# Left rows of a linear attention in full 128-partition tiles, with the first weights' loads moved into the attention

## The chip, the cores and the metric

The kernel runs on one core of one Trainium2 chip. The metric is the device time of one execution in microseconds; times are medians of several executions, and one further execution was taken with the hardware profiler.

## What is computed

```
kv  = einsum('bhsd,bhse->bhde', k, v)          # b 4, h 8, s 576, d 64, all f32
out = einsum('bhsd,bhde->bhse', q, kv)
x   = out / sqrt(mean(out*out, -1) + 1e-6) * g_norm
x   = x.transpose(0, 2, 1, 3).reshape(2304, 512)
x   = softplus(x @ w1) @ w2                    # w1 512 x 2048, w2 2048 x 512
out = leaky_relu(x @ w3, 0.01) @ w4            # the same shapes
```

`softplus` and `leaky_relu` stand for the two expressions of the reference. The two layers after the attention are called the MLPs below.

## The kernel before, in words

The attention is worked off in 16 units: unit u is one batch b and one pair of heads (NU = 4 x 4). The 576 rows of a batch are 4 x 128 rows, and 64 rows that are left (RL = 64). For each unit `load` asks for q, k and v of the 512 rows (256 KB each, a ring of five, line 368), and with a batch's first pair for the 64 left rows of all eight heads (128 KB each, a ring of two, line 377). All these loads, and those of the weights, are asked for by SyncE's queue (SP), in one order.

What a unit does on TensorE (PE): `T(u)` transposes q in four 128x128 blocks (line 400) and the left 64 rows (line 404), then sums k-transposed times v over four blocks of 128 rows (line 408) and over the left 64 rows (line 411). Lines 345 and 347 copy q and k to the layout for this, on VectorE (DVE), ScalarE (ACT) or GpSimd (POOL). The sum is masked (line 426, DVE) to `kvm`, the transposed q goes to `qt` (line 358 on DVE, 356 on ACT). `O(u)` multiplies `qt` by `kvm`: four blocks (line 439), and the left rows (line 445). `normal(w)` takes two units together, w = 0 to 7: squares (line 459, ACT), their sums (line 464, DVE), a reciprocal root, and the scaled rows `xn` (four blocks) and `xnl` (left rows, both line 501, DVE). `X(u)` transposes these back (line 523, and line 535 for the left rows) into `xy`, the input of the first MLP.

In the tiles of the left rows everything has 64 partitions: `ldr` and `xnl` are 64 partitions high, line 404 transposes 64 rows with a 64x64 identity, line 411 contracts over 64 partitions, line 445 writes 64 output rows, line 535 transposes 64 rows.

The first MLP's weights arrive as 64-bit numbers that are taken apart by bit operations (`decode_w`, lines 562 to 597, "chunks" of 512 KB) and then split in a high and a low part (`split_pair`, lines 636 to 669). Chunks 0 and 1 make the first pair, 2 and 3 the second. Their products (line 888) are laid between the later units of the attention as soon as four blocks of `xy` are there, and the MLPs' own products (lines 813, 961, 977) follow.

The order on each engine is not written by hand. `Plan` collects all operations with a cost and a due time, which grows with the PE work that was entered before the operation, and at each step gives each engine the operation that can start and is due first. A due time can be set by hand: `due=4 * no + 10` for the first four chunks (line 573). The planner fixes the order; on the chip each engine works its list off in that order and waits for semaphores.

Of the kernel before, what the change touches and what calls it, by code (L numbers as in the profile page):

```python
# [19 lines left out]
class Plan:  # L20
# [15 lines left out]
        self.readers = {}  # L36
        self.pe = 0.0

    def op(self, cost, fn, reads=(), writes=(), due=None):
        o = {"cost": cost, "fn": fn, "succ": [], "n": len(self.ops)}  # L40
        deps = {}
        for k in reads:
            if k in self.writer:
                deps[self.writer[k]["n"]] = self.writer[k]
        for k in writes:
            for d in [self.writer.get(k), *self.readers.get(k, ())]:
                if d is not None:
                    deps[d["n"]] = d
        for k in reads:
            self.readers.setdefault(k, []).append(o)  # L50
        for k in writes:
            self.writer[k], self.readers[k] = o, []
        o["deps"] = list(deps.values())
        for d in o["deps"]:
            d["succ"].append(o)
        o["due"] = self.pe
        if "PE" in cost:
            self.pe += cost["PE"]
        else:
            o["due"] += self.AHEAD  # L60
        if due is not None:
            o["due"] = due
        self.ops.append(o)
        return o

# [66 lines left out]
def linear_attention_two_mlps(  # L132
# [32 lines left out]
    nc = tc.nc  # L165
    B, H, S, D = q.shape
    NT, DM = out.shape
    DFF = w1.shape[1] // 2
    P = 128
    KC = DM // P  # L170
    NF = DFF // P
    RL = S - 4 * P
# [29 lines left out]
    def ring(pool, name, n, shape, dt=F32):  # L202
        return [pool.tile(shape, dt, name=f"{name}{i}") for i in range(n)]

    ident = const.tile([P, P], F32, name="ident")
# [97 lines left out]
    attp = att.__enter__()  # L303
    NLD = 5
    lda = {nm: ring(attp, nm + "a", NLD, [P, 2, 4, D]) for nm in "qkv"}
    ldr = {nm: ring(attp, nm + "r", 2, [RL, H, D]) for nm in "qkv"}
    qp = ring(attp, "qp", 2, [P, 4, 2, D])
    kp = ring(attp, "kp", 2, [P, 4, 2, D])
    qt = ring(attp, "qt", 2, [P, S])
# [1 line left out]
    sq = ring(mstp, "sq", 2, [P, 8, D])  # L311
    sql = ring(mstp, "sql", 1, [RL, 4, D])
    xn = ring(mstp, "xn", 4, [P, 8, D])
    xnl = ring(mstp, "xnl", 2, [RL, 4, D])

    ss = ring(mstp, "ss", 2, [P, 20])
    fa = ring(mstp, "fa", 2, [P, 20])
    fm = ring(mstp, "fm", 2, [P, 20])
    for t_ in ss:
        nc.vector.memset(t_, 1.0)  # L320

    plan = Plan()
    op = plan.op
# [39 lines left out]
    def load(u):  # L363
        b, hp = u // NPAIR, u % NPAIR
        hs = slice(2 * hp, 2 * hp + 2)
        for nm, src in (("q", q), ("k", k), ("v", v)):
            def fn(e, nm=nm, src=src):
                nc.sync.dma_start(  # L368
                    out=lda[nm][u % NLD],
                    in_=src[b, hs, 0:4 * P, :].rearrange("h (p r) d -> p h r d", r=4),  # L370
                )

            op({"S": 0.73}, fn, (), [(nm, u % NLD)])
        if hp == 0:
            for nm, src in (("q", q), ("k", k), ("v", v)):
                def fn(e, nm=nm, src=src):
                    nc.sync.dma_start(
                        out=ldr[nm][b % 2], in_=src[b, :, 4 * P:S, :].rearrange("h p d -> p h d")
                    )

                op({"S": 0.73}, fn, (), [(nm + "r", b % 2)])

    def T(u):
        b, hp = u // NPAIR, u % NPAIR
        h2 = slice(2 * hp, 2 * hp + 2)
        i = u % 2
        for nm, dst in (("q", qp), ("k", kp)):
            copy_to(
                dst[i], lda[nm][u % NLD].rearrange("p h r d -> p r h d"), 512,
                [(nm, u % NLD)], [(nm + "p", i)],  # L390
            )
        p0 = 2 * i if u < U_H else 0
        p1 = p0 + 1
        kv = ps[p1][:, 2 * P:3 * P]
        ql, kl, vl = (ldr[nm][b % 2] for nm in "qkv")
        va = lda["v"][u % NLD]

        def f_t(e, j):
            for r in range(2):
                nc.tensor.transpose(  # L400
                    ps[p0 + j][:, r * P:(r + 1) * P], qp[i][:, 2 * j + r, :, :], ident
                )
            if j == 0:
                nc.tensor.transpose(ps[p0][:, 2 * P:2 * P + RL], ql[:, h2, :], ident[:RL, :RL])  # L404

        def f_kv(e):
            for r in range(4):
                nc.tensor.matmul(  # L408
                    kv, kp[i][:, r, :, :], va[:, :, r, :], start=(r == 0), stop=False
                )  # L410
            nc.tensor.matmul(kv, kl[:, h2, :], vl[:, h2, :], start=False, stop=True)  # L411

        for j in range(2):
            n = (2 * P + RL, 2 * P)[j]
            c0 = (0, 2 * P + RL)[j]
            op(
                {"PE": 0.25}, lambda e, j=j: f_t(e, j),
                [("qp", i)] + ([] if j else [("qr", b % 2)]), [("ps", p0 + j)],
            )
            if j:  # L420
                op(
                    {"PE": 1.1}, f_kv,
                    [("kp", i), ("v", u % NLD), ("kr", b % 2), ("vr", b % 2)], [("ps", p1)],
                )
                op(
                    {"D": 0.22}, lambda e: nc.vector.tensor_tensor(kvm[i], kv, mask, ALU.mult),
                    [], [("ps", p1), ("kvm", i)],
                )
            from_psum(qt[i][:, c0:c0 + n], ps[p0 + j][:, :n], n, p0 + j, [("qt", i, j)])
# [3 lines left out]
    def O(u):  # L433
        i = u % 2
        at_ = (0, P, 2 * P + RL, 3 * P + RL)

        def f_o(e):
            for r in range(4):
                nc.tensor.matmul(  # L439
                    ps[4 + i][:, r * P:(r + 1) * P], qt[i][:, at_[r]:at_[r] + P], kvm[i],  # L440
                    start=True, stop=True,
                )

        def f_l(e):
            nc.tensor.matmul(  # L445
                ps[6][:RL, i * P:(i + 1) * P], qt[i][:, 2 * P:2 * P + RL], kvm[i],
                start=True, stop=True,
            )

        need = [("kvm", i), ("qt", i, 0)]  # L450
        op({"PE": 0.87}, f_o, need + [("qt", i, 1)], [("ps", 4 + i)])
        op({"PE": 0.22}, f_l, need, [("ps", 6)])
        squares(ps[4 + i], ("ps", 4 + i), sq[i], ss[u // 2 % 2][:, 8 * i:8 * i + 8], ("sq", i),
                ("ss", u // 2 % 2, i), P, 8)
# [14 lines left out]
    def normal(w):  # L469
# [18 lines left out]
        def newton(e):  # L488
# [5 lines left out]
        parts = [  # L494
            (xn[2 * i + t], ps[4 + t], m_[:, 8 * t:8 * t + 8], ("ps", 4 + t), ("xn", 2 * i + t), P, 8)
            for t in range(2)
        ] + [(xnl[i], ol, m_[:RL, 16:20], ("ps", 6), ("xnl", i), RL, 4)]
        for x_, o, r_, ok, xk, p, n in parts:
            op(
                {"D": t_d(n * D)},  # L500
# [16 lines left out]
    def X(u):  # L517
        b, hp = u // NPAIR, u % NPAIR
        i = u % 2

        def f_x(e):
            for r in range(4):
                nc.tensor.transpose(  # L523
                    ps[7][:, r * P:(r + 1) * P], xn[u % 4][:, 2 * r:2 * r + 2, :], ident
                )

        cm, cl = (b * S + RL, b * S) if b % 2 else (b * S, b * S + 4 * P)
        op({"PE": 0.44}, f_x, [("xn", u % 4)], [("ps", 7)])
        scaled(xy[:, hp, cm:cm + 4 * P], ps[7], 4 * P, 7, xyk([hp], cm, 4 * P))
        if i == 0:  # L530
            return

        def f_l(e):
            for t in range(2):
                nc.tensor.transpose(  # L535
                    ps[6][:, 2 * P + t * RL:2 * P + (t + 1) * RL],
                    xnl[u // 2 % 2][:, 2 * t:2 * t + 2, :], ident[:RL, :RL],
                )

        op({"PE": 0.11}, f_l, [("xnl", u // 2 % 2)], [("ps", 6)])  # L540
        scaled(
            xy[:, hp - 1:hp + 1, cl:cl + RL],
            ps[6][:, 2 * P:2 * P + 2 * RL].rearrange("p (a n) -> p a n", a=2),
            2 * RL, 6, xyk([hp - 1, hp], cl, RL),
        )

# [3 lines left out]
    def decode_w(F, which, a_reg):  # L550
# [1 line left out]
        src = ((w1, w2), (w3, w4))[ph][which]  # L552

        ri = chunk_no[0] % 2 if chunk_no[0] >= 6 else chunk_no[0] % 2 * 2
        no = chunk_no[0]
        chunk_no[0] += 1
        r, t_ = raw[ri], sqr

# [10 lines left out]
                )  # L569

        rk, tk, ak = r.keys(), [("sqr",)], a_reg.keys()

        op({"S": 1.46}, f_l, (), rk, due=4 * no + 10 if no < 4 else None)
        op(
            {"A": t_a(DM)},
            lambda e: nc.scalar.activation(  # L576
# [22 lines left out]
    def decode_pair(F, which, i):  # L599

        for m in range(2):
            decode_w(F + m, which, half[i][m])
# [426 lines left out]
        {"D": 0.08}, lambda e: nc.vector.tensor_scalar(gcol, graw, -0.5, None, ALU.mult),  # L1029
        [("graw", 0), ("graw", 1)], [("gcol",)],  # L1030
    )
    for f in range(2):
        decode_pair(2 * f, 0, 0)
        split_pair(0, f, True)
    for i in range(NU + XL):
        if i < NU:
            T(i)
            if i + NLD < NU:
                load(i + NLD)
        if i >= XL:  # L1040
            X(i - XL)
            if i - XL == 2 * NPAIR - 1:
                first_blocks()
                decode_pair(0, 1, 0)
        if 1 <= i <= NU:
            O(i - 1)
            if i % 2 == 0:
                normal(i // 2 - 1)
# [103 lines left out]
```

## Time and profile before

| | us |
|---|---|
| median of 3 runs | 844.09 (843.69 to 844.68) |
| the profiled execution, whole | 841.17 |
| its span in the profile | 839.4 |
| PE busy | 824.8 (98%) |
| DVE busy | 578.1 (69%) |
| ACT busy | 447.8 (53%) |
| POOL busy | 65.6 (8%) |

The profiled execution took 841.17 us, 1.8 us more than the span that the profile shows, and 2.9 us less than the median of the runs. An engine's busy time is an average over an attention of some 97 us and MLPs of some 742 us. A busy PE need not be PE at its peak, since the ends of matmuls are modelled; the distance from the start of one matmul to the start of the next is what PE took for it.

### The profile page before, as it was taken

How to read it: one execution, taken by the hardware profiler on the slowest of the kernel's cores; microseconds unless marked ns; L12 is line 12 of the kernel's file. 1: busy time of each engine (PE TensorE's matmuls, PEld its weight loads, DVE VectorE, ACT ScalarE, POOL GpSimd, SP SyncE). 2: the span in 40 equal slices, each digit the busy share in tenths (PEclk: the TensorE clock that was granted, in tenths of full speed). 3: DMA queues.
4: the chain of work that ended last, by engine and by line, in shares of the span. 5: the costliest groups of instructions: out<-in, count | busy, mean ns of one | idle time of the engine just before them, and what ended most of it. 6: DMA issues, size and time to landing. Idle time of an engine off the chain costs nothing.

```text
span 839.4 us, 11949 instructions
## 1 busy us (share of the span) xinstructions
PE 824.8 (98%) x4524; PEld 772.0 (92%) x4524; DVE 578.1 (69%) x928; ACT 447.8 (53%) x725; POOL 65.6 (8%) x116
## 2 busy tenths in 40 slices
PE   6999999999999999999999999999999999999997
PEld 4788999999999999999999988989889889889886
DVE  6887988878468665867688886766378754753342
ACT  4644976866355544555466565565364554453330
POOL 3321000000100100000000000010010010010000
PEclk9999999999999999999999999999999999999999
DMA  9981565376645752764866965764654852543613
GB/s 309 342 271 64 201 244 188 145 251 211 222 135 162 248 204 72 249 202 158 302 209 212 324 252 191 253 221 134 210 168 135 286 176 65 200 152 100 200 51 100
DMA packets 78712, 164.08 MB, mean 195 GB/s; under 512 B 11456, under 2 KB 54208, under 8 KB 78656
## 3 DMA queue, kind: packets, MB, share of 16 engines
q1 hardware_dynamic: 67136, 100.42, 35.7%
q0 software_dynamic: 11520, 62.92, 22.6%
q8 instruction: 35, 0.57, 0.3%
q14 instruction: 21, 0.17, 0.1%
HBM read 132.25 MB, written 31.06 MB: 195 GB/s over the span
## 4 chain that ended last, share of the span: by engine, by line
PE 96%; DVE 1%; DMA 1%; ACT 1%; SPq 0%; issue 0%; ACTq 0%; DVEq 0%
PE ps L813 40%; PE ps L961 24%; PE ps L977 24%; PE ps L439 2%; PE ps L408 2%; PE ps L888 2%; PE ps L400 1%; PE ps L523 1%; DMA qr<-in_q_dram 1%; PE ps L411 1%; PE ps L445 1%; PE ps L404 0%; DVE xy L691 0%; PE ps L535 0%; SPq L368 0%
## 5 line engine op out<-in xcount | busy, mean ns | idle before, releaser
L813 PE MATMUL ps<-ra 128*128 128x384 f32 x1932 | 387.8, 335 | 0.0
L813 PEld LDWEIGHTS ps<-ra 128*128 128x128 f32 x1932 | 342.8, 188 | 14.0
L961 PE MATMUL ps<-rb 128*128 128x384 f32 x1152 | 226.6, 334 | 0.0
L977 PE MATMUL ps<-rb 128*128 128x512 f32 x864 | 224.7, 393 | 0.0
L961 PEld LDWEIGHTS ps<-rb 128*128 128x128 f32 x1152 | 202.1, 188 | 0.0
L921 DVE TENSOR_TENSOR mf<-ps,mf 128x384 f32<-128x384 f32 x138 | 76.7, 556 | 165.6 <-PE ps L813 134.3
L977 PEld LDWEIGHTS ps<-rb 128*128 128x128 f32 x864 | 159.8, 188 | 23.7
L914 ACT ACTIVATE mf<-ps 128x384 f32<-128x384 f32 x138 | 67.8, 492 | 109.4 <-PE ps L813 108.2
L691 DVE TENSOR_TENSOR xy<-ps,xy 128x384 f32<-128x384 f32 (+1 forms) x126 | 77.3, 614 | 29.1 <-PE ps L977 20.8
L796 POOL DMA_DIRECT2D ra<-xscr x80 | 42.8, 536 | 672.3 <-PE ps L813 652.8
L847 DVE TENSOR_TENSOR rb<-mf,rb 128x768 fp32r<-128x768 f32 x96 | 91.3, 951 | 3.9 <-ACT rb L842 3.8
L842 ACT ACTIVATE rb<-mf 128x768 fp32r<-128x768 f32 x96 | 81.3, 847 | 2.7
L719 ACT ACTIVATE ra<-mf 128x768 fp32r<-128x768 f32 x63 | 53.0, 841 | 27.7 <-PE ps L813 26.7
L714 DVE TENSOR_TENSOR ra<-mf,ra 128x768 fp32r<-128x768 f32 x63 | 60.1, 955 | 11.0 <-ACT ra L719 10.7
L834 ACT ACTIVATE mf<-mf 128x768 f32<-128x768 f32 (+1 forms) x48 | 32.8, 683 | 61.6 <-DVE mf L921 61.6
L828 ACT ACTIVATE mf<-mf 128x768 f32<-128x768 f32 (+1 forms) x48 | 33.3, 694 | 45.1 <-DVE mf L921 45.0
L686 ACT ACTIVATE xy<-ps 128x384 f32<-128x384 f32 (+1 forms) x35 | 18.5, 528 | 15.1 <-PE ps L961 10.8
L588 DVE SCALAR_TENSOR_TENSOR sqr<-mf,sqr 128x512 int32<-128x512 int32 x35 | 24.4, 696 | 0.8
L594 DVE SCALAR_TENSOR_TENSOR mf<-mf,sqr 128x512 int32<-128x512 int32 x34 | 24.0, 706 | 0.4
L576 ACT ACTIVATE mf<-mf 128x512 f32<-128x512 f32 x20 | 13.4, 669 | 17.1 <-DMA mf<-in_moe_w_in_dram 13.7
L400 PE MATMUL ps<-ident,qp 128*128 128x128 f32 x64 | 13.3, 306 | 8.6 <-POOL qp L347 7.8
L582 DVE TENSOR_SCALAR sqr<-mf 128x512 int32<-128x512 int32 x34 | 15.4, 453 | 8.1 <-ACT mf L576 7.5
(85 smaller groups left out, 606.6 us busy)
## 6 DMA issues: line engine op xcount, KB each, us to landing
ra<-xscr POOLq DMA_DIRECT2D x80, 768.0 KB, 6.0
mf<-xscr SPq DMA_DIRECT2D x51, 384.0 KB, 5.5
mf<-in_moe_w_in_dram SPq DMA_DIRECT2D x18, 512.0 KB, 4.8
xscr<-ra SPq DMA_DIRECT2D x12, 768.0 KB, 3.8
xscr<-rc SPq DMA_DIRECT2D x12, 768.0 KB, 4.6
mf<-in_moe_w_out_dram SPq DMA_DIRECT2D x17, 512.0 KB, 4.3
lf<-in_moe_w_out_dram SPq DMA_DIRECT2D x15, 512.0 KB, 3.5
xscr<-xy SPq DMA_DIRECT2D x19, 384.0 KB, 4.1
```

Of the source, the lines that this page charges most:

```text
L691: {"D": t_d(n)}, lambda e: nc.vector.tensor_tensor(dst, src, dst, ALU.add),
L714: ENG[e].tensor_tensor(e_[:, 1, :, :], src(), e_[:, 0, :, :].bitcast(F32), ALU.subtract)
L719: {"A": t_a(n)}, lambda e: nc.scalar.activation(e_[:, 0, :, :], src(), AF.Copy),
L796: lambda e: nc.gpsimd.dma_start(out=flat(xe[i]).ap, in_=xscr[7 * tp + i]),
L813: nc.tensor.matmul(o, w_[:, a, c:c + P], e_[:, b, kk, :], start=(not on and kk == 0 and n == 0), stop=(kk == 1 and n == 2), skip_group_che ...
L828: {"A": t_a(n)}, lambda e: nc.scalar.activation(dst(), src(), AF.Softplus),
L842: {"A": t_a(n)}, lambda e: nc.scalar.activation(g[:, 0, :, :], c.ap, AF.Copy),
L847: lambda e: nc.vector.tensor_tensor(g[:, 1, :, :], c.ap, g[:, 0, :, :].bitcast(F32), ALU.subtract),
L914: {"A": t_a(BN)}, lambda e: nc.scalar.activation(c[:, m, :], src, AF.Copy),
L921: lambda e: nc.vector.tensor_tensor(c[:, m, :], src, c[:, m, :], ALU.add),
L961: nc.tensor.matmul(y[:, :BN], w_[m][:, a, js], G_[:, b, m, :], start=(u == 0 and m == 0 and i == 0), stop=(u == 1 and m == 1 and i == 2),)
L977: nc.tensor.matmul(y, G_[:, a, m, js], w_[m][:, b, :], start=(u == 0 and m == 0 and i == 0), stop=(u == 1 and m == 1 and i == 2),)
```

## The change

Two edits. The tiles of the left rows are made 128 partitions high: the upper 64 partitions of the six `ldr` and the two `xnl` are set to zero once at the start, on DVE, and lines 404, 411, 445 and 535 work on 128 partitions, or 128 output rows. The product of line 445 now reads 64 columns of `qt` that belong to another block, so it also waits for the second half of `qt`; the rows that come of them are not used. Second, the decoding and splitting of the first two pairs of chunks are entered with units 1 and 3 of the attention, where before they were entered ahead of unit 0 with due times set by hand.

```
-    def op(self, cost, fn, reads=(), writes=(), due=None):
+    def op(self, cost, fn, reads=(), writes=()):
...
-        if due is not None:
-            o["due"] = due
...
-    ldr = {nm: ring(attp, nm + "r", 2, [RL, H, D]) for nm in "qkv"}
+    ldr = {nm: ring(attp, nm + "r", 2, [P, H, D]) for nm in "qkv"}
...
-    xnl = ring(mstp, "xnl", 2, [RL, 4, D])
+    xnl = ring(mstp, "xnl", 2, [P, 4, D])
...
+    for t_ in [t for n in "qkv" for t in ldr[n]] + xnl:
+        nc.vector.memset(t_[RL:], 0.0)
...
-                        out=ldr[nm][b % 2], in_=src[b, :, 4 * P:S, :].rearrange("h p d -> p h d")
+                        out=ldr[nm][b % 2][:RL], in_=src[b, :, 4 * P:S, :].rearrange("h p d -> p h d")
...
-                nc.tensor.transpose(ps[p0][:, 2 * P:2 * P + RL], ql[:, h2, :], ident[:RL, :RL])
+                nc.tensor.transpose(ps[p0][:, 2 * P:3 * P], ql[:, h2, :], ident)
...
-                ps[6][:RL, i * P:(i + 1) * P], qt[i][:, 2 * P:2 * P + RL], kvm[i],
+                ps[6][:, i * P:(i + 1) * P], qt[i][:, 2 * P:3 * P], kvm[i],
...
-        need = [("kvm", i), ("qt", i, 0)]
-        op({"PE": 0.87}, f_o, need + [("qt", i, 1)], [("ps", 4 + i)])
+        need = [("kvm", i), ("qt", i, 0), ("qt", i, 1)]
+        op({"PE": 0.87}, f_o, need, [("ps", 4 + i)])
...
-                    ps[6][:, 2 * P + t * RL:2 * P + (t + 1) * RL],
-                    xnl[u // 2 % 2][:, 2 * t:2 * t + 2, :], ident[:RL, :RL],
+                    ps[6][:, (2 + t) * P:(3 + t) * P], xnl[u // 2 % 2][:, 2 * t:2 * t + 2, :], ident,
...
-        op({"S": 1.46}, f_l, (), rk, due=4 * no + 10 if no < 4 else None)
+        op({"S": 1.46}, f_l, (), rk)
...
-    for f in range(2):
-        decode_pair(2 * f, 0, 0)
-        split_pair(0, f, True)
     for i in range(NU + XL):
         if i < NU:
             T(i)
+            if i in (1, 3):
+                decode_pair(2 * (1, 3).index(i), 0, 0)
+                split_pair(0, (1, 3).index(i), True)
```

What the planner makes of it is seen at three places. On SP, before, the list began so (qa, ka, va: q, k, v of a unit; qr, kr, vr: the left rows; mf from moe_w_in: a chunk of the first weights):

```order
L562 DMA mf<-in_moe_w_in_dram 128x4x256 x2
L368 DMA qa_97<-in_q_dram 128x2x256
L368 DMA ka_102<-in_k_dram 128x2x256
L368 DMA qa_98<-in_q_dram 128x2x256
L377 DMA qr_112<-in_q_dram 64x8x64
L368 DMA ka_103<-in_k_dram 128x2x256
L368 DMA va_107<-in_v_dram 128x2x256
L377 DMA kr_114<-in_k_dram 64x8x64
```

Now it begins so (line numbers of the changed kernel):

```order
L370 DMA qa_97<-in_q_dram 128x2x256
L370 DMA ka_102<-in_k_dram 128x2x256
L370 DMA qa_98<-in_q_dram 128x2x256
L379 DMA qr_112<-in_q_dram 64x8x64
L370 DMA ka_103<-in_k_dram 128x2x256
L370 DMA va_107<-in_v_dram 128x2x256
L379 DMA kr_114<-in_k_dram 64x8x64
L379 DMA vr_116<-in_v_dram 64x8x64
L370 DMA va_108<-in_v_dram 128x2x256
L562 DMA mf<-in_moe_w_in_dram 128x4x256
```

The two chunks that stood first now stand behind nine loads of the attention (the second of them four places further), and the third and fourth chunk move back as well, behind loads of units 6 and 7.

On DVE the list now begins, behind the constants, with the eight memsets and with four copies of q and k for units 0 and 1, which POOL made before; the decoding of the first chunk, which stood here before, follows some places later:

```order
L320 MEMSET vr_116 64x512
L320 MEMSET vr_117 64x512
L320 MEMSET xnl_133 64x256
L320 MEMSET xnl_134 64x256
L322 MEMSET ss_135 128x20
L322 MEMSET ss_136 128x20
L347 COPY qp_118<-qa_97 128x512
L347 COPY kp_120<-ka_102 128x512
L347 COPY qp_119<-qa_98 128x512
L347 COPY kp_121<-ka_103 128x512
L428 TENSOR_TENSOR kvm_124<-ps_84,mask 128x128
```

On PE the order stays nearly what it was, and the tiles become full. The transposes of unit 4 (left rows in qr_113) and the products of units 2 and 3, before:

```order
L400 MATMUL ps_84<-ident,qp_118 128x128 x2
L400 MATMUL ps_83<-ident,qp_118 128x128 x2
L404 MATMUL ps_83<-ident,qr_113 128x64
L439 MATMUL ps_87<-kvm_124,qt_122 128x128 x4
L439 MATMUL ps_88<-kvm_125,qt_123 128x128 x4
L445 MATMUL ps_89<-kvm_124,qt_122 64x128
```

And now:

```order
L402 MATMUL ps_84<-ident,qp_118 128x128 x2
L402 MATMUL ps_83<-ident,qp_118 128x128 x2
L406 MATMUL ps_83<-ident,qr_113 128x128
L441 MATMUL ps_87<-kvm_124,qt_122 128x128 x4
L441 MATMUL ps_88<-kvm_125,qt_123 128x128 x4
L447 MATMUL ps_89<-kvm_124,qt_122 128x128
```

The transpose of the left rows has 128 columns where it had 64, and the product of the left rows 128 output rows where it had 64. From the first product of line 813 on, the lists of PE, DVE, ACT and SP are the same before and after, apart from line numbers.

## Rows read from the trace of the kernel before

**Rows 1.** The page: its span, and the chain that ended last by engine.
```profile
span 839.4 us, 11949 instructions
PE 96%; DVE 1%; DMA 1%; ACT 1%; SPq 0%; issue 0%; ACTq 0%; DVEq 0%
```

**Rows 2.** Busy time by stretch: start:end, length, busy by engine, clock, DMA share, GB/s.
```profile
7.83:24.31 16.48, 15.87 (x86) 12.44 (x86) 12.91 (x28) 6.10 (x12) 6.20 (x9) 1.00 1.12 350
24.31:52.18 27.87, 27.03 (x188) 21.78 (x188) 23.76 (x52) 18.04 (x39) 9.16 (x14) 1.00 1.07 338
52.18:97.31 45.13, 44.82 (x298) 38.93 (x298) 36.80 (x75) 26.90 (x54) 5.74 (x7) 1.00 0.31 104
97.31:839.40 742.09, 737.03 (x3955) 698.85 (x3954) 501.92 (x766) 393.76 (x617) 42.84 (x80) 1.00 0.57 192
```

**Rows 3.** The instructions in order of time, 0 to 13 us: start, length, engine, line.
```profile
0.74 1.00 SPq L562 DMA_DIRECT2D mf<-in_moe_w_in_dram  x2
0.84 0.17 DVE L208 MEMSET mask<- 128x128 f32 x1 [0.84 <-PEq L1134]
...
1.24 0.11 DVE L210 MEMSET mask<- 64x64 f32 x1
...
1.79 0.51 SPq L368 DMA_DIRECT2D qa<-in_q_dram  x1
...
4.73 0.66 ACT L576 ACTIVATE mf<-mf 128x512 f32<-128x512 f32 x1 [2.71 <-DMA mf<-in_moe_w_in_dram]
...
6.78 1.00 POOL L347 TENSOR_SCALAR qp<-qa 128x512 f32<-128x512 f32 x1 [5.47 <-DMA qa<-in_q_dram]
...
7.83 1.12 PE L400 MATMUL ps<-ident,qp 128*128 128x128 f32 x4 [7.83 <-POOL qp L347]
...
10.94 2.07 PE L408 MATMUL ps<-va,kp 128*128 128x128 f32 x8
```

**Rows 4.** PE alone in order of time, 28.5 to 37.3 us.
```profile
28.52 0.66 PE L523 MATMUL ps<-ident,xn 128*128 128x128 f32 x4
29.01 0.38 PE L400 MATMUL ps<-ident,qp 128*128 128x128 f32 x2
29.32 0.27 PE L404 MATMUL ps<-ident,qr 64*128 64x64 f32 x1
29.52 0.44 PE L400 MATMUL ps<-ident,qp 128*128 128x128 f32 x2
29.80 1.06 PE L408 MATMUL ps<-va,kp 128*128 128x128 f32 x8
30.79 0.49 PE L411 MATMUL ps<-vr,kr 64*128 64x128 f32 x2
31.24 0.66 PE L523 MATMUL ps<-ident,xn 128*128 128x128 f32 x4
...
34.02 0.34 PE L535 MATMUL ps<-ident,xnl 64*128 64x64 f32 x2
34.28 1.16 PE L408 MATMUL ps<-va,kp 128*128 128x128 f32 x8
...
36.87 0.43 PE L445 MATMUL ps<-kvm,qt 128*64 128x128 f32 x2
37.24 0.66 PE L523 MATMUL ps<-ident,xn 128*128 128x128 f32 x4
```

**Rows 5.** DVE by line and shape, 0 to 100 us: count, busy, mean ns.
```profile
L513 DVE TENSOR_SCALAR xy<-ps,gcol 128x512 f32<-128x512 f32 x5 | 3.7, 747 | 1.2 <-PE ps L523 1.0 <-ACT mf L828 0.2
L636 DVE TENSOR_TENSOR mf<-mf 128x256 f32<-128x256 f32 x8 | 3.6, 456 | 0.1
...
L657 DVE TENSOR_TENSOR ra<-mf,ra 128x768 fp32r<-128x768 f32 x2 | 1.9, 944 | 0.0
...
L345 DVE COPY kp<-ka 128x512 f32<-128x512 f32 x1 | 0.4, 414 | 0.0
```

**Rows 6.** PE's waits in the whole execution: us in total, times, longest.
```profile
PE ps L439 <- DVE xn L501: 0.4, 2, 0.3
```

More of the change, by code (lines that the diff above doesn't have):

```diff
@@ L496, in normal @@
             for t in range(2)
-        ] + [(xnl[i], ol, m_[:RL, 16:20], ("ps", 6), ("xnl", i), RL, 4)]
+        ] + [(xnl[i][:RL], ol, m_[:RL, 16:20], ("ps", 6), ("xnl", i), RL, 4)]
         for x_, o, r_, ok, xk, p, n in parts:
@@ L542, in X @@
             xy[:, hp - 1:hp + 1, cl:cl + RL],
-            ps[6][:, 2 * P:2 * P + 2 * RL].rearrange("p (a n) -> p a n", a=2),
+            ps[6][:, 2 * P:4 * P].rearrange("p (a n) -> p a n", a=2)[:, :, :RL],
             2 * RL, 6, xyk([hp - 1, hp], cl, RL),
@@ L554, in decode_w @@
         ri = chunk_no[0] % 2 if chunk_no[0] >= 6 else chunk_no[0] % 2 * 2
-        no = chunk_no[0]
         chunk_no[0] += 1
```

## The prediction

> **What bounds the kernel now.** Start with the page's span and its chain of waits: PE holds 96% of the chain [rows 1], so a change counts by what it does to PE's line of work. Next the busy times by stretch. I cut them at marks of PE's own list: its first matmul (7.83), the first output product after the scaled rows of w = 0 (24.31), the same after w = 3 (52.18), and the first product of line 813 (97.31). Behind 97.31 PE is busy 737.03 of 742.09 us [rows 2], and the lists of PE, DVE, ACT and SP there are the same in both kernels. I take that stretch as unchanged; the question is how much earlier PE reaches it. Ahead of it PE is busy nearly all the time, but DVE is not far off: 23.76 of 27.87 us between w = 0 and w = 3, against 36.80 of 45.13 behind [rows 2]. Up to 24 us the DMA engines are full, 350 GB/s [rows 2]. Last, the start in order of time: PE sits idle for 7.83 us, because the first copy of q waits until 6.78 for its load [rows 3], which SP asks for at 1.79 behind two chunks of weights asked for at 0.74.
>
> A busy PE hides what the left rows cost. In PE's own rows [rows 4] I read the distance from one start to the next, as the reader should. Four full transposes take 29.01 - 28.52 = 0.49 us, 0.122 each. Two full transposes and line 404 take 29.52 - 29.01 = 0.51, though 404 streams only 64 columns; three full ones would be 0.37. From 29.52 two full transposes, eight records of line 408 and two of line 411 take 1.72 us; the eight of line 408 are 30.79 - 29.80 = 0.99 of it, 0.124 each, so twelve full records would be 1.49. Line 445 alone takes 37.24 - 36.87 = 0.37 for two records, 0.12 over two full ones. Line 535 takes 0.26 for two, against 0.24: nothing there.
>
> **The change, part by part.**
>
> *The start.* The loads of unit 0 are now first in SP's list. A load of 512 KB asked for at 0.74 let ACT begin at 4.73 [rows 3]; one of 256 KB asked for then should be there before 4.7. What ends last is then DVE, which now makes the first copies, behind the memsets. A memset of 128 columns takes 0.17 us, one of 64 columns 0.11 [rows 3]: 0.83 ns a column and 0.06 fixed. Six of 512 columns are 6 x 0.49 = 2.9 us, two of 256 are 2 x 0.27 = 0.5; from about 1.35 they end at 4.8, the two small ones behind them at 4.9. The copy takes 0.41 [rows 5]: PE begins at about 5.4 instead of 7.83, 2.4 earlier. Behind that it meets copies at 0.41 each (the third is done at 6.2) and the left rows' load. Line 408 needs the sixth load, 1.44 MB into the list; before, the two chunks and q (1.3 MB) were there at 6.78, so at 350 GB/s that is about 7.2, in time. Ten transposes later, at the slow pace of the start (1.12 us for four at 7.83, against 0.49 at 28.52, with the granted clock shown as 1.00, the 2.4 GHz level, in both stretches [rows 2, 4]), PE is at line 408 at 8.4 instead of 10.94. I take **-2.5 us**; between -0.5 (the loads of units 2 to 4 come late, since DMA is full up to 24 us and two chunks still stand among them) and -4 (memsets at half the price).
>
> *The full tiles.* If a full record costs what full records cost now, line 404 saves 0.51 - 0.37 = 0.14, line 411 1.72 - 1.49 = 0.23, line 445 0.12 where it stands alone. There are 16 of the first and 16 of the second, and line 445 comes in 11 groups: 2.2 + 3.7 + 1.3 = **7.2 us**. About 1.9 of it lies before 24.31 (units 0 to 3), 3.1 between 24.31 and 52.18 (six of 404, seven of 411, five groups), 2.2 behind.
>
> *DVE's share.* The stretch from w = 0 to w = 3 can't shrink below DVE's work. Between the same two instructions DVE's list now has more in it, since the decoding moved back from the idle start: four more of line 636 (4 x 0.456) and one more of line 657 (0.944), less two of line 513 (2 x 0.747) [rows 5]; four short ones cancel. That is +1.3, so 23.76 + 1.3 = 25.0 us of DVE, while PE alone would take 27.87 - 3.1 = 24.8. Some waits of DVE remain in a list that goes back and forth with PE; it idled 4.1 us in this stretch before, and with more decoding to fill in I take 1.5. The stretch becomes 26.5: it saves 1.4 instead of 3.1. The waits of PE for `xn`, 0.4 us in all now [rows 6], would grow to about 1.7 more. Behind w = 3 DVE has 8.3 us of slack, and the 2.2 arrive whole.
>
> *The rest.* POOL loses three copies and has time. The stronger wait of line 445 (both halves of `qt`) costs nothing: line 439 stands ahead of it in the list and needs both anyway. The chunks of the first weights come later, but the first product of line 888 also waits for `xy` of w = 3; the second pair is needed only behind eight such products.
>
> Sum: -2.5 - 1.9 - 1.4 - 2.2 = **-8.0 us**, from 841.17 to 833.2 for an execution like the profiled one. That one lies 2.9 below the median of the runs; against the median, 844.09, it is **836.1**.
>
> *A rule against it.* In the rows, 64 columns of line 404 take longer than a full transpose. The Trainium skill, "TensorE: Matmul & The Clock Gate", section "Step-by-step: what each phase is for", states the reverse tendency: time goes by the columns that stream in. By that rule the wider transposes cost more, a fuller contraction gains nothing, and the time is 843.6 where the rows give 836.1. What it would be here as a mechanism is the first rival.
>
> **The rivals.**
>
> 1. *The gap stays and the wider tile pays.* The trace calls the gaps ahead of the small tiles only idle, so they might hang on something other than the tile's size: the change of bank, or of operand. Then nothing of the 7.2 comes, and 32 transposes (lines 404 and 535) stream 64 more columns. At half a full transpose, 0.061, that is +2.0; with the start's -2.5 the time is 843.6, no change. At the price of a record of line 535 that doubles (0.13 more) it is +4.2: 845.8, slower. It turns slower from 0.08 a record on. Against it: line 408 behind line 400 shows no such gap, with another bank and other operands.
> 2. *DVE becomes the bound all the way from w = 0 to w = 3*, its idle 4.1 us unchanged: 25.0 + 4.1 = 29.1, 1.2 more than before. Then -2.5 - 1.9 + 1.2 - 2.2 = -5.4: 838.7. For it: 85% busy now, and a list that alternates with PE. Against: PE hardly waited for DVE so far [rows 6].
> 3. *DVE hides everything.* -2.5 - 7.2 = -9.7: 834.4; with -4 at the start, 832.9.
> 4. *The start gains little*, because the loads bound units 2 to 4: about -0.5 - 5.5 = -6.0: 838.1.
>
> **How the numbers follow.** The sum 0.50, rival 2 0.16, rival 3 0.14, rival 4 0.08, rival 1 0.12 (0.06 at each price). The likeliest gives 836.1. The range reaches from 832.5 (rival 3 with the better start) to 841.0, past rivals 2 and 4 and half-way to rival 1, whose 0.12 lies outside. About 0.2%, 1.7 us, is what a measurement of this kernel tells from no change. All cases but rival 1 are faster by more: faster 0.87, the same 0.07, slower 0.06.
>
> **What would show it.** In the changed profile PE's first transposes should start at 5 to 6 us, and a memset of 512 columns take about 0.49. The transpose of line 404 (406 in the changed file) should read 128x128 with starts 0.12 apart, two records of line 411 (413) take 0.25, and PE's idle by "issue" around them vanish. The first product of line 813, at 97.31 now, should come near 89.3. PE should wait for `xn` or `kvm` 1 to 2 us more between w = 0 and w = 3. Behind that mark the stretch should stay 742. The prediction is wrong if the small gaps stay, if PE waits for DVE or loads by more than 4 us in all, or if the stretch of the MLPs itself changes length.

## The result and the profile after

The changed kernel takes 831.53 us (median of 4 executions, 830.92 to 834.89) where the kernel before took 844.2 on the same chip: ratio 0.9858, interval 0.9831 to 0.9886; by the medians it is 12.7 us faster. (The ratios of this document weigh all executions and need not be those of two medians.) The direction of the forecast holds; the time lies 4.6 us under the 836.1 and 1.0 under the range.

The kernel before took 840.3 to 841.9 us in 11 of the 45 executions with which the experiments below were compared, and 843.5 to 846.0 in the others.

The profiled execution took 834.89 us. Its page, answering to [rows 1]:

```profile
span 833.1 us, 11958 instructions
...
PE 93%; DMA 3%; DVE 1%; ACT 1%; SPq 0%; issue 0%; POOL 0%; POOLq 0%; ACTq 0%
```

PE still holds the chain, with 93% where it had 96%: it waits more than before. Where it waits is seen in the busy times by stretch, cut at the same marks as [rows 2] (start:end, length, busy by engine with counts, granted clock, DMA share, GB/s), and in one short window of the third stretch:

```profile
5.76:20.92 15.16, 13.58 (x85) 12.08 (x86) 8.71 (x22) 6.04 (x14) 4.28 (x6) 1.00 1.11 316
20.92:45.70 24.78, 22.70 (x188) 20.98 (x188) 22.79 (x55) 18.88 (x43) 11.46 (x14) 1.00 0.98 299
45.70:91.06 45.36, 41.90 (x297) 40.12 (x298) 36.98 (x75) 29.60 (x58) 5.38 (x8) 0.96 0.58 187
91.06:833.10 742.04, 737.04 (x3955) 698.90 (x3954) 502.04 (x767) 393.99 (x618) 42.94 (x80) 1.00 0.57 192
57.00:59.00 2.00, 2.00 (x12) 2.00 (x13) 1.51 (x3) 0.00 (x0) 0.00 (x0) 0.56 1.07 384
```

The stretch of the MLPs is 742.04 us, where it was 742.09: nothing happened there, as forecast. Everything lies ahead of line 812 (813 before), whose first product comes at 91.06 here and at 86.54 in the second profile below, where the forecast had 89.3. The third stretch, 45.36 us, is not typical. The trace in order of time tells why:

```profile
55.15 0.66 ACT L575 ACTIVATE mf<-mf 128x512 f32<-128x512 f32 x1 [3.11 <-DMA mf<-in_moe_w_out_dram]
...
56.87 0.44 PE L402 MATMUL ps<-ident,qp 128*128 128x128 f32 x2 [2.13 <-ACT qt L358]
57.14 1.83 PE L441 MATMUL ps<-kvm,qt 128*128 128x128 f32 x8
```

ACT's list stood behind a weight load for 3.11 us, PE waited 2.13 us for ACT's `qt`, and then its granted clock was down at 0.50, the 1.2 GHz level, for some 3 us (0.56 on average from 57 to 59): eight records of line 441 took 1.83 us, where they take 1.06 at full clock. In a second profile of the same kernel (the first experiment) none of this happened. So I read the change from that one.

What the prediction asked to look at, first the start, answering to [rows 3]:

```profile
1.41 1.02 DVE L320 MEMSET qr<- 64x512 f32 x2
...
5.76 1.70 PE L402 MATMUL ps<-ident,qp 128*128 128x128 f32 x6 [5.76 <-DVE qp L347]
...
9.05 2.07 PE L410 MATMUL ps<-va,kp 128*128 128x128 f32 x8 [0.75 <-DMA va<-in_v_dram]
```

Two memsets of 512 columns take 1.02 us, where the forecast had 0.98, and the first begins at 1.41 instead of 1.35; the eight end at 5.2 instead of 4.9, and PE begins at 5.76. Then it waits 0.75 for `va`, which the forecast had in time. Second the PE rows in the middle, answering to [rows 4]:

```profile
33.48 0.38 PE L402 MATMUL ps<-ident,qp 128*128 128x128 f32 x2
33.70 0.27 PE L406 MATMUL ps<-ident,qr 128*128 128x128 f32 x1
33.80 0.38 PE L402 MATMUL ps<-ident,qp 128*128 128x128 f32 x2
34.02 1.06 PE L410 MATMUL ps<-va,kp 128*128 128x128 f32 x8
34.92 0.39 PE L413 MATMUL ps<-vr,kr 128*128 128x128 f32 x2
35.14 0.60 PE L525 MATMUL ps<-ident,xn 128*128 128x128 f32 x4
```

From start to start, two transposes with line 406 and two more take 34.02 - 33.48 = 0.54 us for five records, 0.108 each; eight of line 410 take 0.90 and two of 413 take 0.22, 0.11 each. The forecast had taken 0.122 to 0.124 as the price of a full record. This is the first hint at the step that failed.

### The profile page after: what moved, and what is told of

It is laid out like the page before. It is cut to its first block, busy times and chain, and to the rows that moved or that the text cites. A ratio compares the mean times of both kernels' runs of the same rounds, so it can differ in the third digit from the quotient of the medians.

```text
span 833.1 us, 11958 instructions
## 1 busy us (share of the span) xinstructions
PE 815.2 (98%) x4524; PEld 772.1 (93%) x4524; DVE 574.9 (69%) x932; ACT 449.8 (54%) x732; POOL 64.8 (8%) x113
## 4 chain that ended last, share of the span: by engine, by line
PE 93%; DMA 3%; DVE 1%; ACT 1%; SPq 0%; issue 0%; POOL 0%; POOLq 0%; ACTq 0%
PE ps L812 40%; PE ps L960 24%; PE ps L976 24%; PE ps L887 1%; PE ps L410 1%; PE ps L441 1%; DMA ka<-in_k_dram 1%; DMA mf<-in_moe_w_out_dram 1%; DMA va<-in_v_dram 1%; DMA qa<-in_q_dram 1%; PE ps L402 0%; PE ps L525 0%; PE ps L413 0%; DVE xy L690 0%; SPq L370 0%
## 5 line engine op out<-in xcount | busy, mean ns | idle before, releaser
L652 ACT ACTIVATE ra<-mf 128x768 fp32r<-128x768 f32 (+1 forms) x18 | 17.2, 953 | 10.0 <-DVE mf L635 4.8
```

## The experiments

Each was compared with the kernel before on the same chip; its median there was 844.1 to 844.2 us over 11 to 17 executions, which lay between 840.3 and 846.0.

### Both kernels once more, unaltered

> The changed kernel once more, unaltered, for a second profile. In the first one PE sat 2.1 us at 54.7 to 56.9 behind a late load of a second-layer chunk, and then ran 3.4 us at half clock. If that is an accident of that execution, this one shows no such gap and its span is 3 to 4 us shorter, 829 to 830; if it belongs to the kernel, the gap is there again and the span is 833. The median should be 831 to 832 either way.

Measured: 830.94 us (830.38 to 831.25), ratio 0.9853, interval 0.9832 to 0.9875. The stretches of its profiled execution (830.38 in whole, span 828.6):

```profile
5.76:19.74 13.98, 12.46 (x86) 10.87 (x86) 9.41 (x22) 6.24 (x14) 4.46 (x6) 1.00 1.10 339
19.74:45.33 25.59, 22.47 (x189) 21.00 (x188) 23.70 (x55) 18.89 (x43) 13.29 (x15) 1.00 1.08 322
45.33:86.54 41.21, 39.86 (x297) 38.45 (x298) 36.92 (x75) 29.61 (x58) 4.22 (x6) 1.00 0.58 190
```

Against [rows 2]: the start 2.07 shorter, the three stretches 2.50, 2.28 and 3.92 shorter, 10.8 in all, where 8.0 was forecast.

> The kernel before once more, unaltered, for a second profile. Its first profiled execution took 841.2, three less than the median of its timed ones. If the three are a matter of the execution (when the clock of PE comes up, at 15.1 us in the first profile, or a stretch at half clock), this profile's first product of line 813 stands elsewhere than at 97.3, by the same amount as the clock's rise or a half-clock stretch differs; the stretch behind it stays 742 unless it holds such a stretch.

Measured: 844.77 us, span 843.0, which is 3.6 us over the first profile of the same kernel. Its stretches:

```profile
7.86:27.91 20.05, 18.69 (x85) 14.62 (x85) 12.71 (x28) 6.12 (x12) 7.25 (x11) 1.00 1.13 331
27.91:55.80 27.89, 27.05 (x189) 21.80 (x189) 22.97 (x52) 18.04 (x39) 7.97 (x12) 1.00 1.05 334
55.80:100.92 45.12, 44.82 (x298) 38.94 (x298) 36.80 (x75) 26.92 (x54) 5.73 (x7) 1.00 0.27 89
```

The last two stretches repeat [rows 2] to 0.02 us. The whole difference lies in the first: 20.05 against 16.48. The reason is in PE's rows, first of the first profile, then of the second:

```profile
10.94 2.07 PE L408 MATMUL ps<-va,kp 128*128 128x128 f32 x8
...
13.67 1.83 PE L408 MATMUL ps<-va,kp 128*128 128x128 f32 x8
...
16.21 1.16 PE L439 MATMUL ps<-kvm,qt 128*128 128x128 f32 x8
```

```profile
14.11 2.07 PE L408 MATMUL ps<-va,kp 128*128 128x128 f32 x8
...
17.46 2.08 PE L439 MATMUL ps<-kvm,qt 128*128 128x128 f32 x8
...
22.60 1.16 PE L408 MATMUL ps<-va,kp 128*128 128x128 f32 x8
```

Eight records take about 2.07 us at first and 1.16 later; the change comes at about 15 us in one execution and about 22 in the other. The clock column shows 1.00 in both, but an experiment below has the same 2.08 in a window where it shows 0.50. So PE runs on its lower level (1.2 GHz) at first, and when that ends differs by some 7 us between these two executions. The profile that I forecast from (841.17 us) had it early; whether the clock is also what spreads the other executions is not shown.

### Each edit alone

Tiles alone: the changed kernel without its move of loads and decoding.

```
-            if i in (1, 3):
-                decode_pair(2 * (1, 3).index(i), 0, 0)
-                split_pair(0, (1, 3).index(i), True)
+    for f in range(2):
+        decode_pair(2 * f, 0, 0)
+        split_pair(0, f, True)
...
+        op({"S": 1.46}, f_l, (), rk, due=4 * no + 10 if no < 4 else None)
```

> The full tiles alone: loads, due times and the order on every engine as before, plus the eight memsets. Theory A (each small tile costs PE a gap ahead of it, one behind it and part of one more, 0.24 us for a transpose of left rows, 0.38 for a product over 64 rows, some 11 us in all): about 11 us less than before, 833. Theory B (the sizes of the prediction, 7.2 us, less what DVE gives back): 5 to 7 less, 837 to 839. Theory C (most of the gain comes from the loads): no more than 3 less.

Measured: 831.45 us (830.74 to 832.51), ratio 0.9863, interval 0.9843 to 0.9883. Loads alone is the kernel before with that move, and with tiles of 64 partitions and no memsets.

> The moved loads and decoding alone: the order of the changed kernel on every engine, with 64-partition tiles and no memsets. Theory A and B: PE starts earlier, at about 5 us or less, and gains 2 to 3 us, 841 to 842, some of it given back where DVE now decodes beside the attention. Theory C: 9 us less or more. If the two edits only work together, both kernels alone stay within 1 us of before.

Measured: 840.2 us (839.1 to 844.39), ratio 0.9973, interval 0.9954 to 0.9991. So the tiles bring 12.7 us and the loads 2 to 4 by themselves (3.9 by the medians, 2.3 by the ratio), but together 13.2: next to full tiles the earlier start is worth about 0.5, less than the spread. Between profiled executions both are smaller: 1.05 for the loads (841.17 and 840.12, the clock up at 15.1 and 15.6 us in their traces) and 9.8 for the tiles (831.40). So a part of what the medians show may come from when the clock rises. The stretches of tiles alone, whose PE begins at 7.91, show where the rest goes:

```profile
7.91:22.15 14.24, 12.47 (x85) 11.22 (x85) 13.20 (x28) 6.11 (x12) 6.81 (x8) 1.00 1.14 330
22.15:46.88 24.73, 22.35 (x188) 20.97 (x188) 23.36 (x52) 17.95 (x39) 10.75 (x15) 1.00 1.06 350
46.88:87.60 40.72, 39.65 (x298) 38.51 (x299) 36.32 (x74) 26.42 (x53) 5.56 (x7) 1.00 0.49 165
```

With the moved loads, PE is 2.4 us earlier at the mark of w = 0 (19.74 against 22.15), loses 0.86 of it up to w = 3 and 0.49 behind.

### Which of the tiles

Only k's and v's left rows full, which is line 411:

```
+    for t_ in [t for n in "kv" for t in ldr[n]]:
+        nc.vector.memset(t_[RL:], 0.0)
...
```

> Only k and v of the left rows in full tiles (the product over 64 rows becomes one over 128, 16 times), everything else as before, the order on every engine as before. Theory A: 16 x 0.38 = 6 us at most, 4 to 6 less, 838 to 840, since a part of each gap is shared with a small tile that remains beside it. Theory B: 16 x 0.23 = 3.7 less, 840.5. If the gaps hang on something other than the tile's rows: no change.

Measured: 837.42 us (837.21 to 838.85), ratio 0.9935, interval 0.9917 to 0.9953. Then only the transposes, lines 404 and 535:

```
-                nc.tensor.transpose(ps[p0][:, 2 * P:2 * P + RL], ql[:, h2, :], ident[:RL, :RL])
+                nc.tensor.transpose(ps[p0][:, 2 * P:3 * P], ql[:, h2, :], ident)
...
```

> Only the two transposes of left rows in full tiles (lines 404 and 535), the products of left rows as before, on 64 partitions and 64 output rows. Theory A, with the distances of single records: line 404 costs 0.20 + 0.20 + 0.165 with its two neighbours where three full ones take 0.33, so 16 x 0.24 = 3.8, and 535 next to nothing: 3 to 4 less, 840 to 841. If the shares of the parts add up, it is what the full tiles alone gained (12.7) less what k and v alone gained (6.7) and less some 2 for line 445: 4. By columns alone (64 more in 32 records): 2 more, 846.

Measured: 837.26 us (836.32 to 841.84), ratio 0.9926, interval 0.9907 to 0.9946. Each edit is worth about 6.8 by the medians, more than even theory A gave (838 to 840 and 840 to 841): the gaps that went make 4.8 and 5.1 of it (as worked out in the section on why the prediction was wrong), and the rest isn't assigned. Each leaves the other's gaps standing. With k and v full, around line 406, still 64 rows:

```profile
28.49 0.38 PE L402 MATMUL ps<-ident,qp 128*128 128x128 f32 x2
28.80 0.27 PE L406 MATMUL ps<-ident,qr 64*128 64x64 f32 x1
29.00 0.44 PE L402 MATMUL ps<-ident,qp 128*128 128x128 f32 x2
29.28 1.06 PE L410 MATMUL ps<-va,kp 128*128 128x128 f32 x8
```

Two full transposes ahead of the small one take 0.31 to its start, 0.09 over 0.22; the small one 0.20 to the next start, 0.09 over 0.11; and the two behind it 0.28, another 0.06. A small tile costs ahead, behind, and still in the record after the next: 0.24 us in all. With the transposes full, line 406 is free and line 413 not:

```profile
32.71 1.06 PE L410 MATMUL ps<-va,kp 128*128 128x128 f32 x8
33.70 0.48 PE L413 MATMUL ps<-vr,kr 64*128 64x128 f32 x2
34.12 1.16 PE L441 MATMUL ps<-kvm,qt 128*128 128x128 f32 x8
```

Line 413 streams 128 columns, and yet 0.10 is lost ahead of it and its two records take 0.42 instead of 0.22; with 0.05 behind, as after the small transpose, that makes about 0.35. Line 445 (447) is small on its other side: `128*64` in its rows, 128 rows in and 64 output rows. Beyond 0.1105 us a record, its own distances lose 1.55 us in all after the clock's rise, in the kernel before and in both of these runs alike, and 0.05 in the changed kernel. So 64 output rows cost as well.

What goes on in a gap is seen in PE's weight loads (PEld), here of the kernel before, beside [rows 4]:

```profile
28.90 0.25 PEld L400 LDWEIGHTS ps<-ident,qp 128*128 128x128 f32 x2
29.32 0.14 PEld L404 LDWEIGHTS ps<-ident,qr 64*128 64x128 f32 x1 [0.17 <-issue]
29.52 0.20 PEld L400 LDWEIGHTS ps<-ident,qp 128*128 128x128 f32 x2
36.87 0.19 PEld L445 LDWEIGHTS ps<-kvm,qt 128*64 128x64 f32 x2
```

Between full tiles a load begins 0.11 us ahead of its matmul (28.90 against 29.01), while the matmul before it still runs. At a small tile, and at the full one behind it, load and matmul begin together (29.32, 29.52 and 36.87 in both): the overlap is gone. The Trainium skill, "TensorEngine Tiling (Array Packing)", section "Key Properties", says that a change of tiling mode drains TensorE. The rows agree with it, with a price of about 0.09 us a change, though they don't say that a tile of 64 rows is such a change of mode.

### Rows or columns

The changed kernel, its transposes made plain products over 128 full rows with the identity's first 64 columns:

```
-                nc.tensor.transpose(ps[p0][:, 2 * P:3 * P], ql[:, h2, :], ident)
+                nc.tensor.matmul(ps[p0][:, 2 * P:2 * P + RL], ql[:, h2, :], ident[:, :RL], start=True, stop=True)
...
```

> The changed kernel, with the left rows' transposes (lines 406 and 537) as plain products of 128 full rows with only the 64 left columns of the identity: the contraction stays full, the streamed columns are 64 as in the kernel before. Each is two records of 64 columns in place of one of 128. Theory (the price of a small tile hangs on its 64 rows): no gaps come back around them, the two records take about 0.11 us together, and the time is 830.5 to 832. Rival (it hangs on the 64 columns, or on any change of size): gaps of 0.09 ahead and behind return at line 406, 16 x 0.2 = 3.5 us, and the time is 834 to 836.

Measured: 832.74 us (831.7 to 833.88), ratio 0.988, interval 0.9852 to 0.9908.

```profile
29.52 0.66 PE L537 MATMUL ps<-ident,xnl 128*128 128x64 f32 x4 [0.92 <-DVE xnl L503]
30.02 1.11 PE L441 MATMUL ps<-kvm,qt 128*128 128x128 f32 x8
...
34.08 0.38 PE L402 MATMUL ps<-ident,qp 128*128 128x128 f32 x2
34.30 0.33 PE L406 MATMUL ps<-ident,qr 128*128 128x64 f32 x2
34.47 0.39 PE L402 MATMUL ps<-ident,qp 128*128 128x128 f32 x2
34.69 1.06 PE L410 MATMUL ps<-va,kp 128*128 128x128 f32 x8
```

There is no gap: two transposes ahead take 0.22, two behind 0.22. So the price hangs on the tile's 64 rows, not on 64 streamed columns; nor on the transpose as such, since the plain product of line 413 paid it too. The time is 0.7 over what was expected, and the records are longer than expected: two of 64 columns take 0.17 together and not 0.11, and at line 537 four take 0.50 here, behind a wait, and 0.39 at 38.68 and 48.78.

### The start: memsets on POOL, and PE kept busy

```
-        nc.vector.memset(t_[RL:], 0.0)
+        nc.gpsimd.memset(t_[RL:], 0.0)
```

> The changed kernel with its eight memsets on POOL, which is idle until 12.7 us, so that DVE can copy q and k as soon as they are there. If the memsets set PE's start, PE begins at about 4.1 us, as it did with the loads alone, 1.7 earlier. If the start is worth its length, 1.5 less than the changed kernel, 829.5. If loads and the clock's rise swallow it, as the small difference between the full tiles alone and the whole change suggests, no difference: within 0.5 of 831.

Measured: 831.9 us (831.62 to 832.04), ratio 0.985, interval 0.9837 to 0.9863. PE begins at 4.31 instead of 5.76, and nothing comes of it. Next, products of the identity ahead of the attention of the changed kernel:

```
+        for _ in range(9):
+            nc.tensor.matmul(ps[7][:, :P], ident, ident, start=True, stop=True)
         plan.run()
```

> The changed kernel with nine products of the identity by itself ahead of everything on PE, from 1.3 to about 5 us, into a bank that nothing reads before it is written anew; they leave PE in time for the first transposes. If the half-clock stretch at the start (to 9.9 us in the second profile of the changed kernel, 12.9 in the first) is what the early start of PE cannot shorten, PE comes to the attention at full clock or reaches it some us earlier, and the time falls by 1 to 3, to 828 to 830. If the start is bound by loads and copies instead, no change.

Measured: 832.09 us (831.39 to 833.73), ratio 0.9855, interval 0.9843 to 0.9868: no gain; PE waited for `va` at line 410 three times, 2.0 us in all. What follows from both: with full tiles, time won at the start turns into waits for loads, DVE and POOL. The same, with fourteen products, in the kernel before:

> The kernel before with fourteen products of the identity with itself put on PE ahead of everything else; their result is not used. Theory (half speed at the start is a price of its own: in the two profiles of the kernel before the clock rose at 15.1 and 21.8 us, and PE's matmuls ahead of that took twice their time, 3.9 and 7.4 us in all): with PE busy from about 1.4 us on the clock rises by 10 us, and the first product of line 813 comes 2 to 5 us earlier, at about 94; time 839 to 842. Rival (as with the changed kernel, where such products left 832.09 against 830.94): other waits take the place, and the time is 843.5 to 844.5.

Measured: 841.71 us (840.03 to 845.96, 10 executions), ratio 0.9986, interval 0.9967 to 1.0005. The median agrees with the theory, but the interval holds no change: inconclusive. The profiled execution (843.36) was one of those that gained nothing, and shows the clock's work:

```profile
3.00:6.44 3.44, 3.44 (x19) 3.44 (x18) 0.93 (x2) 0.99 (x2) 0.00 (x0) 1.00 1.05 358
6.44:10.00 3.56, 1.93 (x14) 1.43 (x14) 3.35 (x5) 1.02 (x3) 2.14 (x4) 0.98 1.14 338
10.00:14.00 4.00, 3.89 (x15) 2.92 (x15) 3.64 (x8) 1.01 (x2) 1.17 (x2) 0.50 1.11 326
```

The added products, 28 records, took 5.80 us from 1.36 on, 0.21 each, so PE ran on its lower level in the first row too, although the column shows 1.00; in the trace the clock came up at 6.44. From there to 10 us PE was idle for almost half of the time, waiting for POOL and for the left rows of q, and from 9.85 its clock is at 0.50 until it rises again near 20 us. In this stretch eight records of line 408 took 2.08 us.

### The decoding put later

The first two pairs entered with units 3 and 5, then with 5 and 7, instead of 1 and 3:

```
-            if i in (1, 3):
+            if i in (3, 5):
```

> The changed kernel with the decoding and splitting of the first two pairs of chunks entered with units 3 and 5 in place of 1 and 3; a part of DVE's work leaves the stretch from w = 0 to w = 3, and no chunk stands among the loads of units 2 and 3. Theory (what the full tiles give back goes to DVE's work and to loads in this stretch, some 8 us of waits ahead of line 813): the waits for the scaled rows, for va and for qr shrink by 1 to 3 us and the time is 828 to 830. Rival (the work is only moved behind w = 3, where products of line 888 then wait for the weights): 831 or slower, with waits of line 888 for the split weights.

> The same, entered with units 5 and 7. Theory: the stretch from w = 0 to w = 3 is freer still, but now the first pair of weights is due soon after its loads; if DVE's work is what costs, the time lies within 1 us of that with units 3 and 5. Rival: the products of line 888 wait for the weights by 3 us or more, and the time is 833 or slower.

Measured: 832.14 us (831.07 to 833.7), ratio 0.9874, interval 0.9853 to 0.9895; and 832.91 us (830.62 to 834.19), ratio 0.9881, interval 0.986 to 0.9903. Neither is better than the change, and the times that the theory gave don't come. PE's waits in the execution (total, times, longest), first of the changed kernel's second profile, which answers to [rows 6], then of units 5 and 7:

```profile
PE ps L537 <- DVE xnl L503: 1.4, 1, 1.4
PE ps L410 <- DMA va<-in_v_dram: 1.1, 2, 0.7
```

```profile
PE ps L402 <- ACT qt L358: 3.0, 3, 1.5
PE ps L525 <- ACT qt L358: 1.6, 1, 1.6
```

The waits for `va` go away, as hoped, but others for ACT's `qt` take their place. The stretches of the same execution with units 5 and 7, up to the mark of w = 3 and from there to line 812:

```profile
18.22:41.77 23.55, 20.98 (x183) 20.24 (x183) 21.56 (x52) 18.33 (x40) 10.35 (x13) 1.00 1.10 353
41.77:87.83 46.06, 42.26 (x311) 40.12 (x310) 42.16 (x84) 36.97 (x72) 7.85 (x8) 1.00 0.66 225
```

So the stretch from w = 0 to w = 3 did shrink with DVE's work, from 25.59 to 23.55, but the one behind it grew from 41.21 to 46.06 (some 1.0 of it are six records that moved ahead of the mark of line 812). The rival was right that what is won up to w = 3 is lost behind it, but not for its reason: line 887 waits for the weights by at most 0.2 us. This profiled execution (830.62) lies 2.3 under its median, so its waits need not be those of the median.

## Why the prediction was wrong in size

To set the sum against the runs I split PE's time ahead of line 813 by start-to-start distances, over the same 570 records: 0.1105 us for each record (0.1735 for the products of line 888) as the full rate, what goes beyond it by up to 0.16 as small excess, what goes beyond that as waits, and the excess up to the clock's rise on its own. Both limits are choices of mine; the sum doesn't hang on them. The kernel before is that of the rows ahead of the prediction, the changed one its second profile.

| us | before | changed | difference | forecast |
|---|---|---|---|---|
| PE's first matmul | 7.83 | 5.76 | -2.1 | -2.5 |
| excess ahead of the clock's rise | 3.9 | 1.9 | -2.0 | 0 |
| small excess | 14.0 | 2.1 | -12.0 | -7.2 |
| waits | 2.9 | 8.2 | +5.2 | +1.7 |
| sum | | | -10.8 | -8.0 |

**The step that failed** is "If a full record costs what full records cost now". I read 0.122 to 0.124 from groups that stood right behind or right ahead of a small tile, so that the small tiles' price was already in what I took for the full rate. At 0.111, [rows 4] give 0.51 - 0.33 = 0.18 for line 404, and 0.28 - 0.22 = 0.06 in the two records behind it: 0.24 instead of 0.14. The ten records of 408 and 411 take 1.44 instead of 1.11, and 0.05 behind: 0.38 instead of 0.23. Times 16 that is 9.9, and line 445 with 0.15 + 0.05 in 11 groups makes 12.1; measured were 12.0. That it agrees so closely is in part luck, since the tiles ahead of the clock's rise are in another line of the table and line 535 is not in the 12.1. The mechanism was right, the term was 4.8 us too small. The experiments bear out its parts: with line 411 alone full the small excess falls by 4.8, with the transposes alone by 5.1, and with all tiles by 12.6, line 445 among them.

**What DVE gives back** was forecast as 1.7 between w = 0 and w = 3, and nothing behind. There PE's small excess shrank by 5.05 and its waits grew by 2.8 (1.33 to 4.10): the stretch is 25.59 long, where 26.5 was forecast, with DVE busy for 23.70 and idle for 1.9 (forecast: 25.0 and 1.5). So DVE was nearly full as argued, while PE without its waits needs only 21.5 now; but DVE's work did not grow. The added instructions came (eight of line 635 where there were four), and others in the stretch became shorter (two of line 593 took 1.3 us, where they had taken 1.8 as line 594). Behind w = 3 "the 2.2 arrive whole" failed twice: 5.3 came, and 1.4 went to new waits. The waits are for DVE, loads, POOL and ACT in turn. Behind the start those for DVE and loads make 3.3 us in the first profile and 4.2 in the second, about the 4 us that the prediction named as a sign of being wrong. Moving work or loads moved them from one to another. What bounds the attention now, beyond that no single one of these edits frees it, stays open.

**The start** came nearly as forecast in the trace (-2.1 where -2.5 was taken), but is worth 0.5 at most once the tiles are full: tiles alone take 831.45, tiles and loads 830.94 and 831.53 in two comparisons. This was rival 4's claim, for its reason in part (loads), and it mattered little.

**The clock's rise** was no term of the sum. It makes 2.0 us of the profile's difference, and probably the offset: I added 2.9 us, by which the first profiled execution lay under its median, to the changed kernel too. That one lies 0.6 under its median (830.38 against 830.94). The forecast missed this second median by 5.2: 2.8 in the sum, 2.4 in the offset. Each of the two errors of the offset and the tiles' term is by itself more than the 1.0 by which the time left the range, and the tiles' was mostly hidden by waits that grew by 3.5 more than forecast. That the offset comes from the clock was seen in one pair of profiles; an experiment on it was inconclusive. Against the second profile of the kernel before the same split gives -2.1 for PE's first matmul, -5.5 for the clock, -11.1 for the small excess and +4.4 for waits, 14.4 in all. So against that execution, which lies near the median, more than a third of the gain goes with an earlier rise of the clock. The traces have the clock up at 9.6 to 13.6 us in all eight profiles with 128 rows in the transposes and no added products, and at 15.1 to 21.8 us in the four with 64; that the full tiles are what brings it up earlier is not shown beyond that.

**The rivals.** Rival 1 fell: the gaps went with the 64 rows and stayed with them, and a wider transpose costs no more than a small one among its gaps. The rule that stood beside it, time by streamed columns, doesn't hold between these records: 64 columns over full rows took 0.17 for two at line 406 and 0.39 for four at line 537, 0.09 to 0.10 each, 128 columns 0.11. Rival 2 fell too: DVE's idle time went from 4.1 to 1.9. Rival 3's 834.4 (832.9 with the better start) came nearest, but not for its reason, as waits tripled. The likeliest case was right in kind, and its range too narrow at the lower end, since every bound of the tiles' term rested on the same wrong rate, and every bound of the time on the same offset.

## What to carry to other kernels

Read the full rate of an engine from a place where nothing irregular stands within several instructions, or a group's average hides the very price that one looks for. A small tile among full ones costs ahead of it, behind it and a little further: padding it with zeros to full rows can be worth more than the rows that it saves. And where a kernel's start varies between executions, take a second profile of it before you add the distance between the profiled execution and the median to a forecast: the changed kernel need not have that distance.

## What was not expected of the hardware

- Around a tile of 64 rows among full ones each side costs about 0.09 us and a further 0.05 to 0.06 falls on records behind it, with 64 as with 128 streamed columns; a tile of 64 output rows costs as well. At such a tile, and at the full one behind it, the weight load begins together with its matmul and not 0.11 us ahead.
- In two executions of the same kernel the clock came up at about 15 and about 22 us, 7 and 14 us after PE's first matmul, at a cost of 3.6 us in all. The clock column reads 1.00 in both; the spacing of records shows it.
- The granted clock also fell in the middle of the attention, to 0.50 for some 3 us, after PE had waited 2.13 us.
- Plain f32 products of 64 columns gain little over those of 128: 0.17 for two at line 406, 0.39 for four at line 537, where one of 128 columns takes 0.11.
